# Row maxima at the end of a section: moving a small VectorE step, doubling a temporary and re-timing loads in a fused attention and Fourier kernel

## The chip, the cores and the metric

The kernel runs on one core of a Trainium2 chip. The core has five engines, each with its own in-order instruction stream: TensorE (PE in the profile, with its weight loads as PEld), VectorE (DVE), ScalarE (ACT), GpSimd (POOL) and SyncE (SP, which here only issues DMA transfers). They meet through semaphores. The metric is device time in microseconds (us), the median of several runs.

## The reference

Two branches read the same `x` of 2048 x 512, and a gate mixes them row by row.

```python
g = sigmoid((x * gate_w).sum(-1))
a = dft_seq_re @ (x @ dft_hid_re.T) - dft_seq_im @ (x @ dft_hid_im.T)   # Fourier branch
q, k, v = split(x @ wqkv)                     # 32 heads of 16
b = softmax(q @ k.T / 4) @ v @ wo             # attention branch
out = g * a + (1 - g) * b
```

All of it is fp32. The inputs `wqkv` and `wo` are scaled up by 64, so that scores are large and softmax needs the true maximum of each row.

## The kernel before, in words

**Precision.** Products that need fp32 accuracy are made of three fp32r products: each operand is split into a high part (a cast to fp32r) and a low part (the value minus the high part).

**Attention.** Heads go in 16 pairs `p`; the queries of a pair go in two halves `hf` of 1024. A pair's `q` and `k` lie as two stacks of 64 rows in SBUF (`qs`, `ks`, two buffers each, used by even and odd pairs), loaded from DRAM by `load_stacks(p)`: for each of the two heads one transfer of zeros (more for the first pairs) and six transfers of 16 rows. Rows 48 and 49 of a stack hold the high and low part of the negated row maximum, which thus enters the score through the product itself. So every score tile is made twice. First `a_tile` (L290, L292) makes a tile of 128 queries x 512 keys, and VectorE reduces it to a maximum per query. When all 64 tiles of a pair's half are done, two functions go into the list `deferred`: `m_parts` (L301, L304, L305) reduces the four maxima per query to one (`nm`) and splits it into high and low (`nhl`: a cast, then a subtraction); `m_rows` (L309, L315) transposes them and sends them with eight small DMAs to rows 48 and 49 of the stack, four on the SP queue and, in most halves, four on the POOL queue. Later `scores` (L786, L787) makes the tile the other way round, keys x queries, with the maximum in it, and ScalarE takes the exponential into `pt`. `pv` (L828) multiplies with the values into the bank `acc`; where a section ends, `evacuate` copies `acc` (ScalarE) to the tile `few` and adds it on POOL into `total` (L807, L808).

**Fourier.** The second DFT (`dft`, L461) runs 3072 half-height products whose matrices come in chunks `craw` (L435), split by POOL into `ch` and `cl` (L445, L446). Chunk loads, splits, and the `y`, `yr` transfers of finished tiles are issued from `dft_next`, behind the product after which they become possible.

**Order.** The order on each engine is written by hand. A `segment` (called section in the text) walks through a pattern of slots. In the main stage, here called the full stage, the pattern is `FULL`: sixteen slots, each with a half-height DFT product beside a half-height score product of the other half of the array, eight of them `a` and eight `s`, with bank numbers, and then two steps of `pv`.

```python
FULL = "a5 s4 a2 s0 a3 s6 a5 s4 s1 s0 s2 a6 a3 a4 s5 a1 | |"
```

Bank 6 is the bank of `acc`: the `a6` of slot 11, the fifth maximum tile of the section, is reduced before the section's value products may write there. Before the full stage the sections follow `START` and `THIN`, after it `NINE`. `deferred` is emptied one function at a time: in a FULL section at slot 8 (the condition `n == 8`) and at the section's end; in other sections at the end, and in `NINE` also at the first `|`.

Side work hangs on a plan: `at(u, f)` runs `f` when `u` units (a unit is one key tile of a pair's half, two per section) of values are done. It holds `load_stacks(p)` at 32 (p - 1), and `block`, which fetches four finished pairs of a half and their reciprocal sums (`no`, L596, L598), multiplies them (L610, POOL), splits the product (L614, L615, POOL) and stores it (`oh`, L616), all in three steps at 16, 20 and 22 units after the last pair, and the same 8 units later for the second part. At the end `load_w15` fetches some rows of `wo`.

Of the kernel before, what the change touches and what calls it, by code (L numbers as in the profile page):

```python
# [9 lines left out]
F32 = mybir.dt.float32  # L10
F32R = mybir.dt.float32r
AF = mybir.ActivationFunctionType
ALU = mybir.AluOpType
AX = mybir.AxisListType

P = 128
S = 2048
D = 512
# [13 lines left out]
def mix_kernel(ctx: ExitStack, tc: tile.TileContext, xa_t, xa, wqkv, w_hid, w_seq, wo, gate_w, out):  # L32
# [5 lines left out]
    nc = tc.nc  # L38
# [55 lines left out]
    nm = [const.tile([P, 16], F32, name=f"nm{i}") for i in range(2)]  # L94
# [4 lines left out]
    acc = psO.tile([P, 512], F32, "acc")  # L99
# [161 lines left out]
    qs = [main.tile([P, S], F32R, name=f"qs{i}", tag=f"qs{i}") for i in range(2)]  # L261
    ks = [main.tile([P, S], F32R, name=f"ks{i}", tag=f"ks{i}") for i in range(2)]

    def load_stacks(p):
        q_t, k_t = qs[p % 2], ks[p % 2]
        for h in range(2):
            rows = slice((2 * p + h) * DH, (2 * p + h + 1) * DH)
            o = 64 * h
            if p:
                n = 64 if p < 3 else 50  # L270
                nc.sync.dma_start(q_t[o + 48:o + n].bitcast(F32), z_d[:n - 48])
                if p < 3:
                    nc.sync.dma_start(k_t[o + 50:o + 64].bitcast(F32), z_d[:14])

            for i, (qv, kv) in enumerate(((0, 0), (0, 1), (1, 0))):
                part = slice(o + 16 * i, o + 16 * i + 16)
                nc.sync.dma_start(q_t[part].bitcast(F32), qk_d[0][qv, rows])
                nc.sync.dma_start(k_t[part].bitcast(F32), qk_d[1][kv, rows])


    deferred = []
    a_left = {}

    def a_tile(i, h, ps=None, bank=None):
        p, j = divmod(i, 64)
        qt, kb = divmod(j, 4)
        if ps is None:
            ps = psA.tile([P, 512], F32, "a", bank)
        r = slice(64 * h, 64 * h + (64 if p else 48))
        nc.tensor.matmul(ps, qs[p % 2][r, qt * P:(qt + 1) * P], ks[p % 2][r, kb * 512:(kb + 1) * 512],  # L290
                         start=True, stop=True)
        user = nc.vector.tensor_reduce(mx[p % 2][:, h, qt, kb:kb + 1], ps, AX.X, ALU.max)  # L292
        hf = j // 32
        a_left[p, hf] = a_left.get((p, hf), 64) - 1
        if not a_left[p, hf]:
            deferred.extend((partial(m_parts, p, hf), partial(m_rows, p, hf)))
        return user

    def m_parts(p, hf):

        nc.vector.tensor_reduce(nm[hf].rearrange("p (q h) -> p h q", h=2), mx[p % 2][:, :, 8 * hf:8 * hf + 8, :],  # L301
                                AX.X, ALU.max, negate=True)
        t = nhl[hf]
        nc.vector.tensor_copy(t[:, 0], nm[hf])  # L304
        nc.vector.tensor_tensor(t[:, 1], nm[hf], t[:, 0].bitcast(F32), ALU.subtract)  # L305

    def m_rows(p, hf):

# [17 lines left out]
    nc.gpsimd.memset(zeros, 0.0)  # L326
    nc.gpsimd.memset(vt[:, :, :, 16:17], 1.0)
    load_stacks(0)
    wos = [staged(wo[:, kt]) for kt in range(KT)]
    for i in range(2):  # L330
# [93 lines left out]
    work = ctx.enter_context(tc.tile_pool(name="work", bufs=1, side="right", reuse_waits="tile"))  # L424
# [223 lines left out]
    few = work.tile([P, D], F32, name="few")  # L648
# [43 lines left out]
    w15 = []  # L692

    def load_w15():
        w = work.tile([P, 2, D], F32R, name="w15")
        for i in range(8):
            nc.sync.dma_start(w[16 * i:16 * i + 16].bitcast(F32), wo_d[3][64 * (i % 2) + 3:64 * (i % 2) + 64:4])
        w15.append(w)
# [72 lines left out]
    total = None  # L771
# [17 lines left out]
    def pv_last(u):  # L789
# [6 lines left out]
        if blk == 0 and k2 == 7:  # L796
            last_pairs.append(LastPair(0, [(psS, "s"), (psA, "a")]))
            last_pairs[0].copy(1)

    def evacuate(p, hf, done):  # L800

        nonlocal total
        if total is None:
            total = work.tile([P, 512], F32, name="oe", bufs=2)
            nc.scalar.copy(total, acc)
        else:
            nc.scalar.copy(few, acc)  # L807
            nc.gpsimd.tensor_tensor(total, total, few, ALU.add)  # L808
        if done:
            for qb in range(2):  # L810
                nc.sync.dma_start(o_d[hf][p, :, qb * 512:(qb + 1) * 512], total[64 * qb:64 * qb + 64])
            total = None
# [36 lines left out]
    def issue(x, half, stop=True):  # L849
        chain, st, mv, after, last = x  # L850
        i = chain.mm(st, mv, half, last and stop)
        if stop and after:
            after()
        return i
# [12 lines left out]
    def at(u, f, *args):  # L867
        plan.setdefault(u, []).append(partial(f, *args))

    for hf in range(2):  # L870
        for ct in range(4):
            n = 3 if hf and ct == 3 else 4
            last = 32 * (4 * ct + n - 1) + 16 * (hf + 1)
            at(last + (4 if ct < 3 else 2), sums, hf, ct, n)
            at(last + (12 if ct < 3 else 4), inverse, hf, ct, n)
            if ct < 3:
                for half in range(2):
                    for step, du in enumerate((16, 20, 22)):
                        at(last + du + 8 * half, block, step, hf, ct, half)

    for p in range(1, NP):
        at(32 * (p - 1), load_stacks, p)
    one, two, three = [(psD, "d")], [(psS, "s"), (psD, "d")], [(psS, "s"), (psA, "a"), (psD, "d")]
    at(456, load_yg, 0, range(3))
    at(481, load_yg, 0, range(3, 8))
# [2 lines left out]
    for step, u in ((0, 498), ("sums", 500), (1, 504), (2, 506)):  # L888
        at(u, last_block, step, 0, 4, nc.gpsimd)
    at(498, load_w15)  # L890
    lead = a_next

# [11 lines left out]
    FULL = "a5 s4 a2 s0 a3 s6 a5 s4 s1 s0 s2 a6 a3 a4 s5 a1 | |"  # L904
# [14 lines left out]
    users, valued, exponentials = [], 0, []  # L919

    def score(kind, h, number=None):
        x = next(streams[h][kind == "a"], None)
        if x:
            users.append((kind, a_tile(*x, bank=number) if kind == "a" else scores(*x, number=number)))
            if kind == "s":
                exponentials.append(users[-1][1])

    def values(close=False):
        nonlocal valued
        i = pv(valued, close)  # L930
        valued += 1
        return i

    def segment(pattern, half, ds, stop):


        nonlocal users
        before, users = users, []
        ds, turned = iter(ds), False
        for n, slot in enumerate(pattern.split()):  # L940
            number = None
            if n == 8 and pattern == FULL and deferred:
                deferred.pop(0)()
            if slot[1:].isdigit():
                slot, number = slot[0], int(slot[1])
            if slot == "|":
                end = n == len(pattern.split()) - 1
                i = values(end and (pattern == FULL or valued == thin))
                if end and pattern == FULL:

                    tc.add_manual_dep(i.ins, exponentials[-2].ins.name,
                                      mybir.DependencyInfo(mybir.DependencyClass.Sync, mybir.DependencyReason.DATA))
                while between:
                    between.pop(0)()
                if deferred and pattern in NINE and not turned and "|" in pattern.split()[n + 1:]:
                    deferred.pop(0)()
                    turned = True
                continue
            if not n and number is not None:

                score(slot, 1 - half, number)
            if len(slot) == 1:
                x = next(ds, None)
                if x:

                    before = before if x[0].begun else None
                    i = issue(x, half, stop)
                    users = []
                    if before:
                        tc.add_manual_dep(  # L970
                            i.ins, dict(before).get("s", before[0][1]).ins.name,
                            mybir.DependencyInfo(mybir.DependencyClass.Sync, mybir.DependencyReason.DATA))
                        before = None
            if slot != "-" and (n or number is None):
                score(slot[-1] if slot[0] == "+" else slot[0], 1 - half, number)
            if len(slot) == 2 and slot[0] != "+":
                score(slot[1].lower(), half)

        if deferred and not (pattern in NINE and (turned or len(deferred) == 1)):
            deferred.pop(0)()  # L980

# [16 lines left out]
    pump(hid, 12)  # L998
    ds = take(hid, 12)
    segment(START[0], 0, ds, False)  # L1000
    pump(hid, 12)
    segment(START[1], 1, ds, True)
    values()
    values()
    for patterns, ds in pairs():
        for half in range(2):
            run_plan(valued)
            pattern = FULL if patterns is FULL else patterns[half]
# [69 lines left out]
```

## Time and profile before

| | |
|---|---|
| Median of 3 runs | 1703.19 us (1702.84 to 1703.92) |
| Profiled execution | 1702.28 us, its span 1700.5 us |
| TensorE busy | 1666.7 us, 98% |
| VectorE busy | 1397.7 us, 82% |
| ScalarE busy | 1242.7 us, 73% |
| POOL busy | 656.9 us, 39% |
| Row-maximum tile reductions (L292) | 2026 from `a` banks, mean 683 ns, and 22 from `acc` |
| Row-maximum steps (L301, L304, L305) | 32, of these 24 in the full stage |

Times in the timeline are microseconds from the span's start. A row of the timeline is: start, length, engine, line, operation, output and inputs, shapes, and the number of merged instructions; in square brackets stands how long the engine was idle before it, and who ended that. In the chain of work that ended last a row is start, length, and what ran. In the waits, a row gives total, number of times, longest. Busy times of TensorE are modelled from starts, since its products are pipelined, so its 98% doesn't mean that it runs at its peak.

### The profile page before, as it was taken

What the parts mean: (1) busy time and instruction counts of PE and PEld (TensorE: products, weight loads), DVE (VectorE), ACT (ScalarE), POOL (GpSimd) and SP (SyncE); (2) the same over time, 40 slices, a digit from 0 to 9 for tenths busy, and PEclk for the clock granted to TensorE, in tenths of its full rate; (3) what the DMA queues carried; (4) which work ended last, traced back from release to release, by engine and by line L of the source; (5) the groups of instructions that cost most, each with busy time, mean ns of one, the idle gap of its engine ahead of it and who ended that gap; (6) DMA issues with size and microseconds to landing.
All of it is one profiled execution on the core that took longest, in us unless ns stands there. A gap on an engine that the chain in (4) does not pass through costs nothing.

```text
span 1700.5 us, 34533 instructions
## 1 busy us (share of the span) xinstructions
PE 1666.7 (98%) x13040; PEld 1014.8 (60%) x13040; DVE 1397.7 (82%) x2353; ACT 1242.7 (73%) x2423; POOL 656.9 (39%) x672
## 2 busy tenths in 40 slices
PE   9999999999999999999999999999999999999998
PEld 7888855555565556555556555665555555655444
DVE  5439888888888888888888888888888888889854
ACT  5212377777788778777788777877778787788786
POOL 0201112334444456444444465544445465421110
PEclk9999999999999999999999999999999999999999
DMA  9963600414141433314156434314141535452014
GB/s 289 345 150 131 169 11 2 68 33 83 56 77 46 78 109 90 77 43 83 39 95 243 96 101 108 75 54 86 51 83 62 104 101 114 137 182 44 22 44 138
DMA packets 82688, 166.69 MB, mean 98 GB/s; under 512 B 19664, under 2 KB 20158, under 8 KB 78510
## 3 DMA queue, kind: packets, MB, share of 16 engines
q1 hardware_dynamic: 78282, 163.53, 37.7%
q8 instruction: 103, 1.69, 0.4%
q0 software_dynamic: 3808, 0.30, 0.2%
q14 instruction: 63, 0.52, 0.1%
q10 hardware_dynamic: 432, 0.66, 0.1%
HBM read 109.14 MB, written 54.65 MB: 96 GB/s over the span
## 4 chain that ended last, share of the span: by engine, by line
PE 90%; DVE 7%; DMA 2%; issue 0%; POOL 0%; SPq 0%; ACT 0%; DVEq 0%; POOLq 0%
PE acc L828 27%; PE d L461 21%; PE a L290 16%; PE s L786 14%; DVE mx L292 5%; PE s L375 3%; PE s L407 1%; DVE nhl L304 1%; PE acc L794 1%; PE d L375 1%; DMA ks<-qk 1%; DMA craw<-w_seq 1%; PE s L108 1%; PE a L108 1%; PE a L107 1%; PE s L107 1%
## 5 line engine op out<-in xcount | busy, mean ns | idle before, releaser
L292 DVE TENSOR_REDUCE mx<-a 128x1 f32<-128x512 f32 x2026 | 1258.2, 683 | 193.5 <-PE a L290 166.9
L787 ACT ACTIVATE pt<-s 128x512 f32<-128x512 f32 x2006 | 1023.1, 623 | 70.7 <-PE s L786 57.9
L290 PE MATMUL a<-ks,qs 64*128 64x512 f32 (+1 forms) x2026 | 726.3, 404 | 1.1 <-DVE mx L292 1.1
L786 PE MATMUL s<-qs,ks 64*128 64x512 f32 (+1 forms) x2006 | 690.8, 401 | 3.1 <-ACT few L807 3.1
L461 PE MATMUL d<-xab,ch 64*128 64x512 f32 x2016 | 645.7, 395 | 0.0
L828 PE MATMUL acc<-pt,vt 128*17 128x512 f32 (+1 forms) x3968 | 486.6, 598 | 21.7 <-DVE mx L292 21.7
L290 PEld LDWEIGHTS a<-ks,qs 64*128 64x128 f32 (+1 forms) x2026 | 366.4, 184 | 221.3 <-issue 139.8
L808 POOL TENSOR_TENSOR oe<-oe,few 128x512 f32<-128x512 f32 x169 | 218.3, 1292 | 491.3 <-ACT few L807 483.0
L786 PEld LDWEIGHTS s<-qs,ks 64*128 64x128 f32 (+1 forms) x2006 | 365.1, 185 | 65.2 <-issue 16.8
L461 PE MATMUL d<-xab,cl 64*128 64x512 f32 x1008 | 398.3, 395 | 0.0
L461 PEld LDWEIGHTS d<-xab,ch 64*128 64x128 f32 x2016 | 366.8, 184 | 26.5
L807 ACT COPY few<-acc 128x512 f32<-128x512 f32 x169 | 99.1, 587 | 209.5 <-PE acc L828 200.7
L828 PEld LDWEIGHTS acc<-pt,vt 128*17 128x17 f32 (+1 forms) x3968 | 91.6, 101 | 236.7 <-issue 151.6
L461 PEld LDWEIGHTS d<-xab,cl 64*128 64x128 f32 x1008 | 185.8, 184 | 13.2
L446 POOL TENSOR_TENSOR cl<-craw,ch 128x512 fp32r<-128x512 f32 x126 | 162.3, 1288 | 10.1
L445 POOL CAST ch<-craw 128x512 fp32r<-128x512 f32 x126 | 76.9, 611 | 55.9 <-PE s L786 20.3
L461 PE MATMUL d<-wre,xab 64*128 64x512 f32 x336 | 91.4, 404 | 0.0
L461 PEld LDWEIGHTS d<-wre,xab 64*128 64x128 f32 x336 | 58.7, 185 | 38.3 <-issue 23.3
L315 POOL DMA_DIRECT2D qs<-mt x119 | 67.0, 568 | 33.4 <-PE a L290 12.1
L461 PE MATMUL d<-wo_hl,o_hl 64*128 64x512 f32 (+1 forms) x246 | 69.0, 410 | 0.0
L479 POOL CAST xab<-y 128x512 fp32r<-128x512 f32 x16 | 9.8, 611 | 138.9 <-ACT y L477 95.4
L461 PEld LDWEIGHTS d<-wo_hl,o_hl 64*128 64x128 f32 (+1 forms) x246 | 42.1, 185 | 29.8 <-issue 12.2
(170 smaller groups left out, 1055.3 us busy)
## 6 DMA issues: line engine op xcount, KB each, us to landing
craw<-w_seq SPq DMA_DIRECT2D x128, 256.0 KB
qk<-hl SPq DMA_DIRECT2D x32, 512.0 KB
qs<-qk SPq DMA_DIRECT2D x96, 128.0 KB
ks<-qk SPq DMA_DIRECT2D x96, 128.0 KB
b<-hl SPq DMA_DIRECT2D x16, 512.0 KB
xab<-b SPq DMA_DIRECT2D x16, 512.0 KB
o<-oe SPq DMA_DIRECT2D x62, 128.0 KB
oh<-nh SPq DMA_DIRECT2D x12, 512.0 KB
```

What stands on the lines that cost most here:

```text
L290: nc.tensor.matmul(ps, qs[p % 2][r, qt * P:(qt + 1) * P], ks[p % 2][r, kb * 512:(kb + 1) * 512], start=True, stop=True)
L292: user = nc.vector.tensor_reduce(mx[p % 2][:, h, qt, kb:kb + 1], ps, AX.X, ALU.max)
L315: (nc.gpsimd if own else nc.sync).dma_start(rows.rearrange("v (q b c) -> v b q c", q=8, b=4)[:, b], mt[hf][32 * b + h:32 * b + 32:2])
L375: i = nc.tensor.matmul(ps, st[r], mv[r], start=not half and not j, stop=half == 1 and j == 11)
L445: nc.gpsimd.tensor_copy(h1, raw)
L446: nc.gpsimd.tensor_tensor(l1, raw, h1.bitcast(F32), ALU.subtract)
L461: i = nc.tensor.matmul(self.ps, st[r], mv[r], start=not self.begun, stop=stop)
L786: nc.tensor.matmul(ps, ks[p % 2][rr, kt * P:(kt + 1) * P], qs[p % 2][rr, q0:q0 + 512], start=True, stop=True)
L787: return nc.scalar.activation(pts[u][:, 2 * qb + h], ps, AF.Exp, bias=0.0, scale=DH ** -0.5)
L807: nc.scalar.copy(few, acc)
L808: nc.gpsimd.tensor_tensor(total, total, few, ALU.add)
L828: i = nc.tensor.matmul(acc[32 * j:32 * j + width], v[:, 16 * h:16 * h + width], pt[:, j], start=begin, stop=done or close)
```

## The change

Four edits are made together.

1. In FULL sections both deferred functions, `m_parts` and `m_rows`, are run at the section's end; the place at slot 8 is gone. In these sections the high part is made on VectorE by a `tensor_tensor` that takes the maximum of `nm` with itself, in place of a cast. In all other sections the cast and the subtraction are issued on POOL.
2. `evacuate` copies `acc` into two temporaries in turn, `part[0]` and `part[1]`, in place of the one tile `few`. They lie in the buffer that `w15` takes at the end.
3. `load_stacks` is called for one head at a time; the second head of a pair is fetched 2 units after the first (not for the first call, `p` = 1).
4. The three steps of `block` are planned 4 units later: 20, 24 and 26.

```diff
-    def load_stacks(p):
+    def load_stacks(p, heads=range(2)):
         q_t, k_t = qs[p % 2], ks[p % 2]
-        for h in range(2):
+        for h in heads:
...
         t = nhl[hf]
-        nc.vector.tensor_copy(t[:, 0], nm[hf])
-        nc.vector.tensor_tensor(t[:, 1], nm[hf], t[:, 0].bitcast(F32), ALU.subtract)
+        if full_now:
+            nc.vector.tensor_tensor(t[:, 0], nm[hf], nm[hf], ALU.max)
+        else:
+            nc.gpsimd.tensor_copy(t[:, 0], nm[hf])
+        (nc.vector if full_now else nc.gpsimd).tensor_tensor(t[:, 1], nm[hf], t[:, 0].bitcast(F32), ALU.subtract)
...
     def load_w15():
-        w = work.tile([P, 2, D], F32R, name="w15")
+        part.clear()
+        w = work.tile([P, 2, D], F32R, name="w15", tag="w15")
...
         else:
-            nc.scalar.copy(few, acc)
-            nc.gpsimd.tensor_tensor(total, total, few, ALU.add)
+            if not part:
+                two = work.tile([P, 2, 512], F32, name="part", tag="w15")
+                part.extend(two[:, i] for i in range(2))
+            part.reverse()
+            nc.scalar.copy(part[0], acc)
+            nc.gpsimd.tensor_tensor(total, total, part[0], ALU.add)
...
-                    for step, du in enumerate((16, 20, 22)):
+                    for step, du in enumerate((20, 24, 26)):
                         at(last + du + 8 * half, block, step, hf, ct, half)
 
     for p in range(1, NP):
-        at(32 * (p - 1), load_stacks, p)
+        for h in range(2):
+            at(32 * (p - 1) + 2 * h * (p > 1), load_stacks, p, [h])
...
     def segment(pattern, half, ds, stop):
-        nonlocal users
+        nonlocal users, full_now
+        full_now = pattern == FULL
...
-            if n == 8 and pattern == FULL and deferred:
-                deferred.pop(0)()
...
+        while full_now and deferred:
+            deferred.pop(0)()
         if deferred and not (pattern in NINE and (turned or len(deferred) == 1)):
             deferred.pop(0)()
```

More of the change, by code (lines that the diff above doesn't have):

```diff
@@ L281, in mix_kernel @@
     deferred = []
+    full_now = False
     a_left = {}
@@ L798, in pv_last @@
             last_pairs[0].copy(1)
+    part = []
     def evacuate(p, hf, done):
```

## The prediction

> **What bounds the kernel now.** I read the page first, for the engines' shares and the chain that ended last; then the timeline of VectorE and of TensorE, section by section; then the row-maximum tiles, POOL and the chain in order of time.
>
> ```profile
> span 1700.5 us, 34533 instructions
> PE 1666.7 (98%) x13040; PEld 1014.8 (60%) x13040; DVE 1397.7 (82%) x2353; ACT 1242.7 (73%) x2423; POOL 656.9 (39%) x672
> ...
> PE 90%; DVE 7%; DMA 2%; issue 0%; POOL 0%; SPq 0%; ACT 0%; DVEq 0%; POOLq 0%
> ```
>
> TensorE is the bound, with VectorE in the chain for 7%. Where VectorE enters shows in its timeline; each full section is one row of eight reductions (L292, one per score tile).
>
> ```profile
> 601.30 2.48 DVE L292 TENSOR_REDUCE mx<-a 128x1 f32<-128x512 f32 x4 [0.68 <-PE a L290]
> 603.82 0.22 DVE L301 TENSOR_REDUCE nm<-mx 128x16 f32<-128x64 f32 x1
> 604.07 0.82 DVE L304 CAST nhl<-nm 128x16 fp32r<-128x16 f32 x1
> ...
> 605.37 2.47 DVE L292 TENSOR_REDUCE mx<-a 128x1 f32<-128x512 f32 x4
> ...
> 608.49 5.04 DVE L292 TENSOR_REDUCE mx<-a 128x1 f32<-128x512 f32 x8 [0.53 <-PE a L290]
> ...
> 648.77 2.48 DVE L292 TENSOR_REDUCE mx<-a 128x1 f32<-128x512 f32 x4 [0.71 <-PE a L290]
> ...
> 655.00 5.04 DVE L292 TENSOR_REDUCE mx<-a 128x1 f32<-128x512 f32 x8 [0.53 <-PE a L290]
> 660.76 5.04 DVE L292 TENSOR_REDUCE mx<-a 128x1 f32<-128x512 f32 x8 [0.72 <-PE a L290]
> ...
> 695.37 2.48 DVE L292 TENSOR_REDUCE mx<-a 128x1 f32<-128x512 f32 x4 [0.72 <-PE a L290]
> ...
> 702.23 5.04 DVE L292 TENSOR_REDUCE mx<-a 128x1 f32<-128x512 f32 x8 [0.53 <-PE a L290]
> ```
>
> An ordinary section lasts 5.76 us (655.00 to 660.76) and leaves VectorE 0.72 us idle at its end. One section in eight also carries the row-maximum step (L301, L304, L305) between its fourth and fifth reduction, and lasts 7.19 us (601.30 to 608.49), 6.23 (648.77 to 655.00) or 6.86 (695.37 to 702.23). The step delays the fifth reduction, whose bank the value products (L828) accumulate into next, so TensorE waits. The three lengths come from the cast:
>
> ```profile
> L304 DVE CAST nhl<-nm x32: 174/784/836, 172.4 to 1636.9; 128x16 fp32r<-128x16 f32 x32
> L305 DVE TENSOR_TENSOR nhl<-nm,nhl x32: 174/176/518, 172.6 to 1637.5; 128x16 fp32r<-128x16 f32 x32
> ```
>
> ```profile
> 603.57 1.29 POOL L446 TENSOR_TENSOR cl<-craw,ch 128x512 fp32r<-128x512 f32 x1
> ```
>
> A cast of 16 columns takes 174 ns at best and 784 in the median. The one at 604.07 ended at 604.89, 0.03 after POOL's subtraction (604.86): it waited for POOL.
>
> Two of these sections are longer still:
>
> ```profile
> 975.14 1.92 PE L828 MATMUL acc<-pt,vt 128*32 128x512 f32 x16
> 983.91 1.93 PE L828 MATMUL acc<-pt,vt 128*32 128x512 f32 x16 [0.78 <-DVE mx L292]
> ```
>
> ```profile
> 363.64 1.85 PE acc L828 x16
> ...
> 962.70 6.68 DMA ks<-qk
> 969.46 6.72 DMA craw<-w_seq
> ...
> 1490.56 1.85 PE acc L828 x16
> ```
>
> ```profile
> 976.30 0.61 POOL L445 CAST ch<-craw 128x512 fp32r<-128x512 f32 x1 [7.37 <-DMA craw<-w_seq]
> ```
>
> ```profile
> 979.54 0.58 ACT L807 COPY few<-acc 128x512 f32<-128x512 f32 x1 [3.49 <-POOL oe L808]
> ```
>
> 8.77 us from products to products. The DFT chunk `craw` was issued behind fourteen stack loads and landed late, POOL stood 7.37 us, its addition that frees `few` came late, and ScalarE stood 3.49 us. The second, four head pairs later, looks the same.
>
> Summed over the full stage: 24 sections with the step, twelve near 1.10 above 5.75, four near 1.44, six near 0.49, two near 3.05: 13.2 + 5.8 + 2.9 + 6.1 = 28.0 us. Check: from 363.64 to 1490.56 are 191 sections, 1126.92 us, against 191 x 5.75 = 1098.3 (28.7 over; 26.8 with 5.76). So nothing but these 24 sections is over.
>
> **The change, part by part.** The sum is made against the profiled execution, 1702.28 us (its span of 1700.5 and 1.8 around it), 0.9 below the median of 1703.19.
>
> *Step at the section's end, max in place of the cast (24 sections).* Removed from mid-section: everything that makes the 28.0. Added behind the eighth reduction: L301 (0.22), the max, the subtraction, then the transposition that stands there already and takes 0.19 of the idle time (0.72 against 0.53). No max of 16 columns is in the trace; its nearest row is L305, the same form and size: 0.17, or 0.52 where POOL holds it up. I take 0.17. With three gaps of 0.03 that is 0.19 + 0.22 + 0.17 + 0.17 + 0.09 = 0.84 against 0.72: the next section's first reduction starts 0.12 late. Does that reach TensorE?
>
> ```profile
> 803.77 1.44 DVE L292 TENSOR_REDUCE mx<-a 128x1 f32<-128x512 f32 x2
> ```
>
> ```profile
> 805.31 0.64 PE L828 MATMUL acc<-pt,vt 128*32 128x512 f32 x4
> ```
>
> These are the fourth and fifth reductions of an ordinary section. Back to back they run 0.60 apart (2.48 for four of 0.68), so the fifth could end at 803.77 + 0.60 + 0.68 = 805.05; it ended at 805.21, having waited for its matmul, and the products followed 0.10 later, where a delayed fifth is followed in 0.05. About 0.2 us in hand covers 0.12. Without the cover each section costs 0.12, 3 us in all.
>
> The row transfers (L315; eight issues a step, four on POOL behind its addition) leave the 0.7 us later that the transposition comes; the maxima are gathered several sections before they are read.
>
> *What POOL still does to the step.* Where the DFT's second half ends a chain, POOL works at the section's end:
>
> ```profile
> 1031.02 1.92 PE acc L828 x16
> ```
>
> ```profile
> 1032.70 0.61 POOL L445 CAST ch<-craw 128x512 fp32r<-128x512 f32 x1
> ```
>
> Counted from the start of a section's products, the eighth reduction ends at 1.70 (805.21 + 3 x 0.60 = 807.01, against 805.31), so the max is due at 1.96; this cast runs from 1.68 to 2.29, and a max that waits for it ends at 2.32, not 2.13. That is 0.19 late on top of the 0.12, of which the 0.2 in hand leaves about 0.1. By the instruction order of the changed kernel four or five of the 24 are like this, and in one a delayed block product pushes POOL's work back, so that the max and the subtraction both wait: 1.3 late, 1.1 after the cover. Residue: 1.1 + 5 x 0.1, and some rounding: 2.0. Full stage: 28.0 - 2.0 = 26.0 gained.
>
> *Two temporaries, halved stacks, later blocks.* The 2 x 2.0 us of the long sections beyond 1.1 are in that 28.0. In the new order `craw` stands behind seven stack loads, not fourteen and four block loads: about 5 us earlier, and a late addition finds a second buffer. All other full sections are level, so these edits gain nothing there. Their cost: the second half's seven issues move one section behind the first's (5.75 later, in place of seven issues of about 0.5, so some 2.3 us), past `craw`, `yr` and sometimes an `oh` store on SP.
>
> ```profile
> 968.60 0.30 SPq L278 DMA_DIRECT2D ks<-qk  x1
> ```
>
> ```profile
> 985.77 0.50 PE L290 MATMUL a<-ks,qs 64*128 64x512 f32 x1
> ```
>
> The last stack load of pair 9 was issued at 968.60, lands in about 6.7, and its first user runs at 985.77: 10.5 in hand, 8 after the change. Zero. Blocks move by two sections on queues with room; they are read hundreds of us later. Zero.
>
> *Step outside the full stage (8 of 32): cast and subtraction on POOL.*
>
> ```profile
> 230.28 1.05 PE L828 MATMUL acc<-pt,vt 128*17 128x512 f32 x8
> 234.76 1.05 PE L828 MATMUL acc<-pt,vt 128*17 128x512 f32 x8
> 236.88 1.05 PE L828 MATMUL acc<-pt,vt 128*17 128x512 f32 x8
> 240.48 1.05 PE L828 MATMUL acc<-pt,vt 128*17 128x512 f32 x8
> ...
> 1502.28 1.05 PE L828 MATMUL acc<-pt,vt 128*17 128x512 f32 x8
> 1506.19 1.05 PE L828 MATMUL acc<-pt,vt 128*17 128x512 f32 x8
> ...
> 1513.79 1.05 PE L828 MATMUL acc<-pt,vt 128*17 128x512 f32 x8
> 1517.11 1.05 PE L828 MATMUL acc<-pt,vt 128*17 128x512 f32 x8
> ```
>
> ```profile
> 238.34 0.20 DVE L309 STREAM_TRANSPOSE mt<-nhl 128x32 f32<-128x32 f32 x1
> ```
>
> Before the full stage three steps cost 4.48 - 3.60 = 0.88 each, where they put 1.1 on VectorE; only L301 with its gap (0.25) remains, about what is absorbed today. Gain 3 x 0.85 = 2.6 (bounds 0 and 2.6). After it, three cost 3.91 - 3.32 = 0.59 for 0.6 on VectorE; 0.25 remains: gain 3 x 0.3 = 0.9 (0 to 1.8). The two others, at 172 and 1637: 0.2 and 0. POOL's price for 16 columns is not in the trace; it lies between nothing and the 512-column rows, 0.61 + 1.29 = 1.9, and the transposition that waits for it comes 3.6 us after the products of its section began (238.34 against 234.76). Only at 1637 does it follow at once: 0 to 1.9, and what it feeds is read some steps later. I take 0.
>
> Sum: 26.0 + 2.6 + 0.9 + 0.2 = 29.7 us. 1702.3 - 29.7 = 1672.6; on the median's level 1673.5. Forecast: **1673 us**.
>
> **The rivals.**
> *The wait moves along with the step.* The max reads SBUF twice and, like L305 at its 518 ns, can be held up by a POOL instruction. A full wait of 1.29 per section, less 0.1 still in hand, gives 1.2; in all 24 sections that is 29 and the time about 1702, in half 14 and 1687. For it: the row above. Against: in most of these sections POOL's row ends before the step would begin. Chance 0.09.
> The Trainium skill (SBUF — State Buffer, the section "SBUF: two separate sides") says that a VectorE instruction with two SBUF inputs takes the port pair shared with GpSimd against a GpSimd instruction that reads SBUF, as a two-port copy does. By that rule swapping the cast for a max avoids nothing, and only the place can help; the 518 ns agree.
>
> *The two long sections stay*, because another load takes the place of the stacks ahead of `craw` (the blocks now follow them): 2 x 2.0 back, 1677. Chance 0.11.
>
> *POOL is slow with the small operations* outside the full stage and gives those 3.7 back: 1676 to 1677. Chance 0.05.
>
> *Slower: the second half stack comes too late.* It now stands on SP behind `craw`, whose issue waits for POOL.
>
> ```profile
> SPq L435 <- POOL cl L446: 431.6, 98, 11.1
> ```
>
> These waits run up to 11.1 us. Past the 8 in hand, each microsecond stops TensorE once for each of 14 pairs: at 10.1 late the 29.7 are used up, at 11.1 the time is 1673 + 14 x 3.1 = 1716. Against: most such waits end before the second half is due at all. Chance 0.04.
>
> **How the numbers follow.** Forecast 0.71, rivals 0.09, 0.11, 0.05, 0.04. A measurement of this kernel can tell about 0.2%, 3.4 us, from no change; only the last rival and the far end of the first are not faster: faster 0.94, same 0.02, slower 0.04. Range: below, all excess gone (28.0 + 2.6 + 1.8 + 0.4 = 32.8): 1670, a little less for scatter, 1668. Above: the long sections stay and half a dozen steps wait: 1673 + 4 + 6 x 1.2 = 1684.
>
> **What would show it.** Right: sections with the step at 5.75 to 5.9, the new max near 0.17, no row of L828 that waits over 0.5 for VectorE, no 8.8 us section, ScalarE never waiting for POOL's addition. Wrong: a max of 0.5 or more in many sections; TensorE or VectorE waiting for `ks` or `qs` loads; new sections of 7 us or more where blocks meet `craw`.

## The result and the profile after

The changed kernel takes 1674.97 us (median of 4 runs, 1674.52 to 1675.48) against 1703.28 us for the kernel before on the same chip (1702.84 to 1703.92): a ratio of 0.9834, with a 95% interval of 0.9817 to 0.9851. The forecast was 1673, its range 1668 to 1684. The profiled execution took 1675.2 us, its span 1673.4, which is 27.1 less than before.

Lines have moved by the edits: what was L290, L292, L301, L304, L305, L309, L828 is now L291, L293, L302, L306, L309, L313, L839. Of the page of the changed kernel, the span, the engines' shares and the chain by engine:

```profile
span 1673.4 us, 34595 instructions
PE 1663.6 (99%) x13040; PEld 1023.8 (61%) x13040; DVE 1383.1 (83%) x2337; ACT 1242.9 (74%) x2423; POOL 660.1 (39%) x688
...
PE 98%; DVE 1%; DMA 0%; ACT 0%; issue 0%; DVEq 0%
```

VectorE's busy time fell by only 14.6 us (1397.7 to 1383.1), but its share of the chain that ended last fell from 7% to 1%. TensorE is now 98% of that chain. The full stage lost 22.2 us, counted from its first full value products to its last:

```profile
359.92 1.92 PE L839 MATMUL acc<-pt,vt 128*32 128x512 f32 x16
...
1464.67 1.92 PE L839 MATMUL acc<-pt,vt 128*32 128x512 f32 x15
```

These are TensorE's timeline rows that answer to the chain rows at 363.64 and 1490.56 before: 1104.75 us against 1126.92. The first of them also comes 3.7 us earlier, which is the gain ahead of the full stage, and the rest, 27.1 - 22.2 - 3.7 = 1.2, lies behind it.

The step at its new place, in VectorE's timeline of the changed kernel:

```profile
597.93 0.21 DVE L302 TENSOR_REDUCE nm<-mx 128x16 f32<-128x64 f32 x1
598.17 0.26 DVE L306 TENSOR_TENSOR nhl<-nm 128x16 fp32r<-128x16 f32 x1
598.47 0.18 DVE L309 TENSOR_TENSOR nhl<-nm,nhl 128x16 fp32r<-128x16 f32 x1
598.77 0.21 DVE L313 STREAM_TRANSPOSE mt<-nhl 128x32 f32<-128x32 f32 x1
598.91 4.87 DVE L293 TENSOR_REDUCE mx<-a 128x1 f32<-128x512 f32 x8
...
604.50 5.05 DVE L293 TENSOR_REDUCE mx<-a 128x1 f32<-128x512 f32 x8 [0.26 <-PE a L291]
```

The step now stands between two rows of eight reductions, in the time that was idle. The section's own row of eight is whole again (4.87 us, without an idle gap in it), and the products that follow this step came 5.77 us after those before it, against 7.19 for the corresponding section before.

The row-maximum operations, by tile (duration in ns: least, median, most):

```profile
L306 DVE TENSOR_TENSOR nhl<-nm x24: 174/175/1041, 367.6 to 1431.0; 128x16 fp32r<-128x16 f32 x24
L309 DVE TENSOR_TENSOR nhl<-nm,nhl x24: 174/175/519, 367.8 to 1432.1; 128x16 fp32r<-128x16 f32 x24
L308 POOL CAST nhl<-nm x8: 190/196/209, 171.9 to 1610.3; 128x16 fp32r<-128x16 f32 x8
L309 POOL TENSOR_TENSOR nhl<-nm,nhl x8: 220/222/223, 172.2 to 1610.6; 128x16 fp32r<-128x16 f32 x8
```

The median of the first is 175 ns where the cast had 784. But the longest max took 1041 ns, more than any cast before. And POOL's small operations cost 0.20 and 0.22 us, together about a fifth of the 1.9 us that the prediction had to set as their bound.

In the waits of the changed kernel (total, times, longest), the weight loads of the value products still wait for VectorE in every section, but by 0.4 at most, and ScalarE's copy waits for the products, by 1.3 at most:

```profile
ACT part L818 <- PE acc L839: 181.1, 166, 1.3
PEld acc L839 <- DVE mx L293: 62.5, 192, 0.4
PE a L291 <- DVE mx L293: 2.2, 4, 0.6
```

Before, the second of these waits was 84.8 us with 1.8 at most, and the value products on TensorE itself waited another 21.7 us for VectorE. The third row is the larger one now (1.1 us before); the next paragraph shows where its four waits come from. No section near 8.8 us is left.

**Where 6.0 us stayed.** The 24 sections with a step exceed 5.75 us by 6.0 in sum, where 28.0 were and 2.0 were expected. Sixteen are over by 0.01 to 0.08 (0.7 in sum), three by 0.22 to 0.26 (their max takes 0.37 to 0.38, until POOL's subtraction L450 ends), one by 0.41, and four by 1.02 to 1.07 (4.2 in sum). One of the four, in the timeline of the changed kernel:

```profile
1011.40 1.93 PE L839 MATMUL acc<-pt,vt 128*32 128x512 f32 x16
1012.96 1.28 POOL L524 TENSOR_TENSOR y<-y,yr 128x512 f32<-128x512 f32 x1
1013.24 1.04 DVE L306 TENSOR_TENSOR nhl<-nm 128x16 fp32r<-128x16 f32 x1
1014.19 0.61 POOL L449 CAST ch<-craw 128x512 fp32r<-128x512 f32 x1
1014.31 0.52 DVE L309 TENSOR_TENSOR nhl<-nm,nhl 128x16 fp32r<-128x16 f32 x1
1014.86 0.21 DVE L313 STREAM_TRANSPOSE mt<-nhl 128x32 f32<-128x32 f32 x1
...
1018.22 1.92 PE L839 MATMUL acc<-pt,vt 128*32 128x512 f32 x16
```

POOL adds a finished Fourier tile (L524, 1012.96 to 1014.24). The max is due at 1013.24 and ends at 1014.28, 0.04 after it. Then POOL's next cast begins at 1014.19, and the subtraction takes 0.52 in place of 0.17. Max and subtraction both wait, 0.87 + 0.35 = 1.22 late, so the reductions behind them are late too, a product of a later maximum tile waits for the bank that they empty (one of the four waits above), and the section lasts 6.82 us.

Sixteen sections are not quite at 5.75 either. Two rows of the same view show why:

```profile
552.30 0.17 DVE L309 TENSOR_TENSOR nhl<-nm,nhl 128x16 fp32r<-128x16 f32 x1
552.71 0.21 DVE L313 STREAM_TRANSPOSE mt<-nhl 128x32 f32<-128x32 f32 x1 [0.23 <-DVE nhl L309]
```

The transposition starts 0.23 us after the subtraction ends, where the prediction reckoned 0.03. Between the two, the trace has four separate wait instructions of VectorE for the transposition's output buffer, which the last row transfers must have left; they are not counted as busy:

```
EVENT_SEMAPHORE L313   552.317
EVENT_SEMAPHORE L313   552.415
EVENT_SEMAPHORE L313   552.513
EVENT_SEMAPHORE L313   552.611
STREAM_TRANSPOSE L313  552.707
```

One takes about 0.1 us, though nothing was left to wait for: the semaphores that these four read had last changed 20 us before or earlier. Before, the same waits stood at 652.26 to 652.55, early in a section and 1.7 us ahead of their transposition (654.28), with reductions in between, so they cost nothing that showed.

### The profile page after: what moved, and what is told of

Same layout as the page of the kernel before. It is cut to its first block, busy times and chain, and to the rows that moved or that the text cites. A ratio compares the mean times of both kernels' runs of the same rounds, so it can differ in the third digit from the quotient of the medians.

```text
span 1673.4 us, 34595 instructions
## 1 busy us (share of the span) xinstructions
PE 1663.6 (99%) x13040; PEld 1023.8 (61%) x13040; DVE 1383.1 (83%) x2337; ACT 1242.9 (74%) x2423; POOL 660.1 (39%) x688
## 4 chain that ended last, share of the span: by engine, by line
PE 98%; DVE 1%; DMA 0%; ACT 0%; issue 0%; DVEq 0%
PE acc L839 27%; PE d L465 27%; PE a L291 17%; PE s L791 14%; PE s L379 3%; PE s L411 1%; PE acc L799 1%; PE d L379 1%; PE s L106 1%; PE a L106 1%; PE a L108 1%; PE s L108 1%; PE s L107 1%; PE a L107 1%; DVE mx L293 1%; PE s L465 1%
## 5 line engine op out<-in xcount | busy, mean ns | idle before, releaser
L293 DVE TENSOR_REDUCE mx<-a 128x1 f32<-128x512 f32 x2026 | 1256.5, 683 | 177.3 <-PE a L291 151.8
L291 PE MATMUL a<-ks,qs 64*128 64x512 f32 (+1 forms) x2026 | 726.7, 405 | 2.2 <-DVE mx L293 2.2
L291 PEld LDWEIGHTS a<-ks,qs 64*128 64x128 f32 (+1 forms) x2026 | 366.3, 184 | 217.2 <-issue 128.7
L839 PE MATMUL acc<-pt,vt 128*17 128x512 f32 (+1 forms) x3968 | 486.7, 598 | 0.0
L819 POOL TENSOR_TENSOR oe<-oe,part 128x512 f32<-128x512 f32 x169 | 218.3, 1292 | 507.7 <-ACT part L818 502.6
L818 ACT COPY part<-acc 128x512 f32<-128x512 f32 x169 | 99.2, 587 | 183.0 <-PE acc L839 181.1
L839 PEld LDWEIGHTS acc<-pt,vt 128*17 128x17 f32 (+1 forms) x3968 | 91.6, 101 | 214.3 <-issue 151.5
L450 POOL TENSOR_TENSOR cl<-craw,ch 128x512 fp32r<-128x512 f32 x126 | 162.1, 1286 | 10.1
L465 PEld LDWEIGHTS d<-wo_hl,o_hl 64*128 64x128 f32 (+1 forms) x246 | 42.3, 185 | 29.7 <-issue 12.1
```

The lines of the kernel that those rows point to most:

```text
L450: nc.gpsimd.tensor_tensor(l1, raw, h1.bitcast(F32), ALU.subtract)
L465: i = nc.tensor.matmul(self.ps, st[r], mv[r], start=not self.begun, stop=stop)
L818: nc.scalar.copy(part[0], acc)
L819: nc.gpsimd.tensor_tensor(total, total, part[0], ALU.add)
L839: i = nc.tensor.matmul(acc[32 * j:32 * j + width], v[:, 16 * h:16 * h + width], pt[:, j], start=begin, stop=done or close)
```

## Experiments

"Over" below is by how much the sections of the full stage exceed 5.75 us in one profiled execution, summed over those with a step and those clearly longer than 5.75: 28.0 before, 6.0 after the change. Each ratio is to the kernel before on the same chip, with its 95% interval.

### The place or the operation

Two kernels split the first edit. One keeps the max and puts the step back into the middle of the section; the other keeps the place and goes back to the cast.

```diff
+            if n == 8 and pattern == FULL and deferred:
+                deferred.pop(0)()
...
-        while full_now and deferred:
-            deferred.pop(0)()
```

> The whole change, but in full sections the step is back at slot 8, with the max in place of the cast. Theory (the place is what counts, and the max waits for POOL like the cast): 14 sections at 1.1, 4 at 1.44 and 6 at 0.5 over the ordinary one, 24 us, against 6.0 in the changed kernel: about 1693 us. Rival (the operation is what counts): the max runs in 0.17 everywhere, each section is over by 0.5 as those with a short cast were, 12 us: about 1681 us.

```diff
-            nc.vector.tensor_tensor(t[:, 0], nm[hf], nm[hf], ALU.max)
+            nc.vector.tensor_copy(t[:, 0], nm[hf])
```

> The whole change, but the high part is made by the cast, as before, at the section's end. Theory (place): as the changed kernel, 1675 us, within 1. Rival (operation): the cast waits at the section's end too and in more sections than the max, 0.5 to 1.2 us in a third of them or more: 1679 to 1690 us.

Max in the middle: 1692.13 us, 0.9940 (0.9924 to 0.9957), 23.5 over. Cast at the end: 1674.91 us, 0.9840 (0.9825 to 0.9855), 6.1 over. The tile's rows, first of the max in the middle, then of the cast at the end:

```profile
L306 DVE TENSOR_TENSOR nhl<-nm x24: 191/824/897, 366.0 to 1446.6; 128x16 fp32r<-128x16 f32 x24
```

```profile
L306 DVE CAST nhl<-nm x24: 174/175/1042, 367.6 to 1431.0; 128x16 fp32r<-128x16 f32 x24
```

In the middle, the max waits as the cast did in the kernel before (824 ns in the median against 784). At the end the cast is as quick as the max, and waits in the same sections. In the middle the max gains nothing either: with the same loads and temporaries, the old cast there leaves 23.5 us over as well (the second run of the next section). So the operation is worth nothing, and the place everything. The Trainium skill (SBUF — State Buffer, the section "SBUF: two separate sides") has it that a VectorE instruction with two SBUF inputs takes the port pair that it shares with GpSimd against a GpSimd instruction that reads SBUF, just as a copy does. These rows agree: 824 ns beside POOL's work, 174 clear of it.

### The step alone, and the other three edits alone

> The moved step alone: row maxima at the section's end with the max, POOL outside the full stage; one temporary, whole stacks, blocks at 16, 20 and 22 as before. Theory: the step is worth all but the two long sections, and these need the other three edits; they come back with about 2 us each, so about 1679 us against 1675 for the whole change. Rival: the long sections were long only because a delayed section met a late addition; without the delay they are ordinary, and the time is 1675.

> The other three edits alone: two temporaries, stacks in halves, blocks 4 units later, with the old step (cast and subtraction on VectorE, at slot 8). Theory: only the two long sections shrink to some 1.1 us of excess, about 1699 us against 1703.3. Rival: the edits move the stall elsewhere or were never the cause, 1703.

The first undoes edits 2, 3 and 4; the second has these and the old step. Step alone: 1682.86 us, 0.9885 (0.9870 to 0.9900), 13.5 over. The others alone: 1696.70 us, 0.9966 (0.9955 to 0.9978), 23.5 over. The first missed by 4 us upwards, the second by 2 downwards. In the kernel with the step alone, the 24 sections with a step are over by 6.0, as in the whole change. The other 7.5 lie in two sections without a step, 3.60 and 3.87 over. The timeline of the kernel with the step alone, at the first of the two:

```profile
960.72 0.61 POOL L449 CAST ch<-craw 128x512 fp32r<-128x512 f32 x1 [7.63 <-DMA craw<-w_seq]
...
963.95 0.58 ACT L814 COPY few<-acc 128x512 f32<-128x512 f32 x1 [3.74 <-POOL oe L815]
...
964.59 0.49 PE L791 MATMUL s<-qs,ks 64*128 64x512 f32 x1 [1.78 <-ACT few L814]
...
968.66 2.20 PE L835 MATMUL acc<-pt,vt 128*32 128x512 f32 x16
```

It is the stall that the prediction found: a late chunk, POOL waiting 7.63, ScalarE 3.74, and then TensorE 1.78 for a score's bank. In the kernel before, the step stood in the same section as this stall and took its delay in the shadow of it, 3.03 and 3.08 over in all. The prediction had split those as 1.1 for the step and 2.0 for the stall. With the step gone the stall shows in full: it was worth 3.6 to 3.9 by itself, and the step there nothing. (POOL's wait is also 0.26 us longer in this run than before, so the two sizes are not quite alike.)

With the other three edits alone, the two long sections fall from 3.03 and 3.08 to 0.84 and 0.83, and that is all but 0.1 of the 4.5 us by which the sum over falls; smaller shifts in the other sections cancel. The full stage of that run also begins 1.2 us earlier than before the change. Of this, 1.05 us is there already where the first row-maximum step begins (171.09 against 172.14 us), before any of the edits acts. In two traces of the changed kernel itself it begins at 171.65 and 171.16 us, and in all 14 traces between 171.1 and 172.6, so most of the 1.2 is scatter of the start.

### Which of the three edits removes that stall

Three kernels have the step's edit and one of the others: the two temporaries, the halved stacks, or the later blocks. Each undoes two of these:

```diff
-            part.reverse()
-            nc.scalar.copy(part[0], acc)
-            nc.gpsimd.tensor_tensor(total, total, part[0], ALU.add)
+            nc.scalar.copy(few, acc)
+            nc.gpsimd.tensor_tensor(total, total, few, ALU.add)
...
-                    for step, du in enumerate((20, 24, 26)):
+                    for step, du in enumerate((16, 20, 22)):
...
-        for h in range(2):
-            at(32 * (p - 1) + 2 * h * (p > 1), load_stacks, p, [h])
+        at(32 * (p - 1), load_stacks, p)
```

> The moved step and the two temporaries, with whole stacks and the blocks as before. Theory: the two long sections are ScalarE's wait for the one temporary; with a second one it is gone, 1675 us, though the chunk still lands late. Rival: POOL is so late that both temporaries are taken, and more than half of the 7.5 us that the two sections cost with the step alone stays: 1679 to 1683.

> The moved step and the stacks in halves, with one temporary and the blocks as before. Theory: the chunk load stands behind seven stack loads less and lands some 3 us earlier, so that about 3 of each section's 3.7 us go: 1676 us. Rival: the four block loads and the first half hold it as long: 1680 or more.

> The moved step and the later blocks, with one temporary and whole stacks. Theory: the chunk load still stands behind fourteen stack loads; only the four block loads ahead of them (2.6 us of issues) and a block product on POOL are out of the way: about 2 of each section's 3.7 us go, 1679 us. Rival: the blocks' work on POOL was the cause: 1675.

With the temporaries 1676.26 us, 0.9843 (0.9828 to 0.9857), 7.6 over; with the stacks 1675.30, 0.9836 (0.9821 to 0.9851), 5.9 over; with the blocks 1675.27, 0.9836 (0.9822 to 0.9851), 6.0 over. Any one of the three does the whole work of the three, within about 1 us. For the first two that is near what was expected. For the later blocks 1679 was expected, and the number of its rival came out. How they do it differs, as POOL's wait for the chunk shows (total, times, longest): first with the temporaries, then with the stacks, then with the blocks.

```profile
POOL ch L449 <- DMA craw<-w_seq: 19.8, 3, 7.3
```

```profile
POOL ch L449 <- DMA craw<-w_seq: 0.8, 1, 0.8
```

```profile
POOL ch L449 <- DMA craw<-w_seq: 5.9, 1, 5.9
ACT few L814 <- POOL oe L815: 4.1, 3, 1.5
```

The halved stacks remove the wait. With the later blocks the 5.9 is a wait elsewhere, at 1236 us, which the kernel with the step alone has too (5.91) and which costs nothing. At the first of the two places POOL now stands 5.95 in place of 7.63, and the trace puts that down to TensorE and no longer to the chunk:

```profile
957.57 0.61 POOL L449 CAST ch<-craw 128x512 fp32r<-128x512 f32 x1 [5.95 <-PE s L791]
```

This split begins some 3 us sooner than with the step alone (960.72), and ScalarE waits for the products alone. At the second place ScalarE waits 1.53 for POOL's addition, and the section is 0.2 over. The rival, that the blocks' work on POOL was the cause, doesn't fit the rows of the step alone, though its number came out: ScalarE's wait of 3.74 ended at 963.95 with the addition, while the block's cast on POOL started at 963.86, behind that addition. The temporaries leave the wait as it is (7.3) and take ScalarE out of it; POOL's backlog then meets two steps (0.28 and 1.12 over, where the changed kernel has 0.01 and 0.02), which is where the extra 1.4 us is.

### POOL for the steps outside the full stage

```diff
-            nc.gpsimd.tensor_copy(t[:, 0], nm[hf])
-        (nc.vector if full_now else nc.gpsimd).tensor_tensor(
+            nc.vector.tensor_copy(t[:, 0], nm[hf])
+        nc.vector.tensor_tensor(
```

> The whole change, but outside the full stage the cast and the subtraction stay on VectorE. Theory: the three steps before the full stage lose their 0.9 us again, the three after it 0.4, the first one 0.4 at most: 3.9 to 4.3 us, 1679 us. Rival: these steps were hidden and the gain there came from elsewhere: 1675.

1679.61 us, 0.9861 (0.9845 to 0.9878): as expected. Timeline rows of the value products around the second such step, of the changed kernel, and then of this one:

```profile
229.39 1.05 PE L839 MATMUL acc<-pt,vt 128*17 128x512 f32 x8
232.94 1.05 PE L839 MATMUL acc<-pt,vt 128*17 128x512 f32 x8
```

```profile
229.39 1.05 PE L839 MATMUL acc<-pt,vt 128*17 128x512 f32 x8
233.86 1.05 PE L839 MATMUL acc<-pt,vt 128*17 128x512 f32 x8
```

3.55 us with the cast and the subtraction on POOL, 4.47 with them on VectorE, at the same place. With POOL the step costs nothing there (the section at 240.79, without a step, takes 3.55 too), although the first reduction of the step is still on VectorE.

### Waiting past POOL's addition

The four sections at 1.05 should go if the step waited for the end of the next section, where POOL has other work.

```diff
+        due = len(deferred)
...
-        while full_now and deferred:
+        for _ in range(due if full_now else 0):
             deferred.pop(0)()
-        if deferred and not (pattern in NINE and (turned or len(deferred) == 1)):
+        if not full_now and deferred and not (pattern in NINE and (turned or len(deferred) == 1)):
```

> The whole change, but in full sections the step waits for the end of the section after the one that ends the maxima: the other half of the pair of sections, in which no DFT chunk is split and no y tile is added. Theory (the 6.0 us that are left in the full stage are POOL instructions that hold up the max and the subtraction): the four sections at 1.05, the one at 0.41 and the three at 0.24 become like the others, 0.05 to 0.1; the row transfers leave 5.75 us later, which the 8 us between their landing and the first score that reads them cover: 1670 us. Rival: the rest is the longer tail of VectorE itself or the later transfers stop TensorE: 1675 or more.

1674.93 us, 0.9833 (0.9816 to 0.9849): no better than the change, a miss of 5 us. The long waits for POOL did go (the max takes 360 ns at most, the subtraction 177), but two others came. In the timeline of this kernel, VectorE at one of seven steps that are over by 0.37 to 0.47, and TensorE in a section that is over by 1.44:

```profile
558.89 0.21 DVE L313 STREAM_TRANSPOSE mt<-nhl 128x32 f32<-128x32 f32 x1 [0.23 <-DVE nhl L309]
559.03 0.52 DVE L582 RECIPROCAL rc<-rc 128x64 f32<-128x64 f32 x1
559.47 3.07 DVE L293 TENSOR_REDUCE mx<-a 128x1 f32<-128x512 f32 x5
...
891.17 0.47 PE L791 MATMUL s<-qs,ks 64*128 64x512 f32 x1 [0.99 <-DMA qs<-mt]
```

The reciprocal of the sums is planned for just that section's end, and it makes the step half a microsecond longer, in six of the seven; the seventh has a gap of 0.58 us ahead of its transposition instead. And one score comes to wait for the rows of maxima, which the later step sends later.

To test the first of these readings, the reciprocal was moved one section on, with the changed kernel run beside it on the same chip:

```diff
-            at(last + (12 if ct < 3 else 4), inverse, hf, ct, n)
+            at(last + (14 if ct < 3 else 4), inverse, hf, ct, n)
```

> The whole change, with two things added: every row-maximum step of a full section waits for the end of the section after the one in which its maxima are complete, and the reciprocal of the sums is planned two units (one section) later, at 14 in place of 12, so that it no longer stands right behind the transposition. With the step waiting alone, eight sections were over by 0.37 to 0.47 with the reciprocal in them, and one by 1.44 where a score waited for a row transfer; the sum over was 5.7 us. Theory (the eight are the reciprocal's): they fall to under 0.1 each, the one of 1.44 stays, the sum over falls to about 2.5 us and the time to 1671.7. Rival (the eight come from the later place of the step itself): they stay, and the time is 1674.9. Second rival: the moved reciprocal now meets something else, a score or another step, and makes new long sections of its own; then the eight are gone, but the sum over stays at 4 us or more.

> The changed kernel as it is, beside the other kernel of this call on the same chip, as the measure for it: 1675.0 by its earlier runs, and 3.3 us slower than the kernel with the step one section later and the reciprocal moved, if that one's theory holds; equal to it within 1 us if the first rival holds.

1672.53 us (1672.31 to 1673.29), 0.9824 (0.9811 to 0.9838), against 1674.50 (1674.29 to 1674.91), 0.9836 (0.9823 to 0.9849) for the changed kernel beside it: 2.0 us faster, where the theory had 3.3. The expectation spoke of eight, by counting one of 0.24 in. The six with a reciprocal fall to below 0.1, so these were the reciprocal's. The one with the gap of 0.58 stays, at 0.44, and so does the one of 0.24. The score's wait stays and is a little longer (1.23, its section 1.70 over). One section with the moved reciprocal is over by 0.36, so the second rival has a small part. 3.8 us remain over.

Last, the step waits only in the second half of the full stage, where the four additions meet it, and the reciprocals move too:

```diff
+        due = len(deferred)
+        late = valued >= thin + 1 + 4 * NT * 3
...
-        while full_now and deferred:
+        for _ in range((due if late else len(deferred)) if full_now else 0):
             deferred.pop(0)()
...
-            at(last + (12 if ct < 3 else 4), inverse, hf, ct, n)
+            at(last + (14 if ct < 3 else 4), inverse, hf, ct, n)
```

> The whole change, and two things more: in the second half of the full stage, from its unit 246 on, the step waits for the end of the next section, as in the earlier run, and the reciprocals of the sums are planned 2 units later, so that they no longer stand behind the step. Theory: the waits for POOL's y additions (four of 1.05, one of 0.41) go, the reciprocals' 0.4 does not come in their place, and the one late transfer of the earlier run (1.4) stood in the first half: 4.3 us less, about 1671 us. Rival: other instructions or transfers meet the step there: 1673 to 1675.

1671.76 us (1671.19 to 1672.15), 0.9814 (0.9800 to 0.9829), 1.9 over: the lowest median of all, near the expected 1671, though its interval overlaps that of the kernel before it. It wasn't run beside the changed kernel; their times don't overlap, while the kernel before agreed within 0.5 us beside each (1703.77 and 1703.28). Its timeline at the step that was shown at 1013.24 above and now comes one section later:

```profile
1019.62 0.36 DVE L306 TENSOR_TENSOR nhl<-nm 128x16 fp32r<-128x16 f32 x1
1020.01 0.17 DVE L309 TENSOR_TENSOR nhl<-nm,nhl 128x16 fp32r<-128x16 f32 x1
1020.38 0.21 DVE L313 STREAM_TRANSPOSE mt<-nhl 128x32 f32<-128x32 f32 x1 [0.20 <-DVE nhl L309]
```

The max and the subtraction that took 1.04 and 0.52 take 0.36 and 0.17 there.

## Why the prediction was right, and where it was off

The forecast of 1673 missed the median of 1674.97 by 2 us, and its reason held: the mid-section step delayed the fifth reduction, and the place at the end took that away. The number came out somewhat better than the full stage did: that gained 3.8 us less than forecast, and 1.2 us more elsewhere made up for part of it, about 0.5 of this probably luck (the scatter of the start, below). By its own terms, from the two profiled executions:

| Term | predicted | measured |
|---|---|---|
| Ahead of the full stage | 2.6 + 0.2 | 3.7 |
| Full stage | 26.0 | 22.2 |
| After it | 0.9 | 1.2 |
| Sum | 29.7 | 27.1 |

*The full stage's 28.0.* The sum was right, and all of it was the 24 sections. Its split was not: the two long sections were not 1.1 for the step and 2.0 for the late chunk, but nearly all the chunk's stall. That changes nothing in the sum, since both went, but it makes the three other edits worth 7.5 us (13.5 - 6.0) beside the new step where 4.0 stood, so that the price of the rival in which those sections stay was too low (1677 where the run without the edits took 1682.9).

*The residue of 2.0 is the term that failed*: 6.0. The step that failed in it is "in one a delayed block product pushes POOL's work back, so that the max and the subtraction both wait", with five others at 0.1. Its price was right (1.1; the rows give 1.02 to 1.07), but it occurs four times, and a block product isn't its cause. What the max meets is POOL's addition of a finished Fourier tile, which starts when ScalarE has handed over the tile `y`. It stands right ahead of the cast at 1032.70 from which the prediction reckoned. Here it is before the change, where the products came at 1031.02, and after it at the second of the four places, where they came at 1150.58 and no block is near:

```profile
1031.48 1.28 POOL L520 TENSOR_TENSOR y<-y,yr 128x512 f32<-128x512 f32 x1 [1.36 <-ACT y L519]
```

```profile
1152.13 1.29 POOL L524 TENSOR_TENSOR y<-y,yr 128x512 f32<-128x512 f32 x1 [1.29 <-ACT y L523]
1152.43 1.02 DVE L306 TENSOR_TENSOR nhl<-nm 128x16 fp32r<-128x16 f32 x1
```

In all four sections the addition began 0.45 to 0.47 us after the products before the change and 1.53 to 1.56 after them now. The prediction placed POOL's work by its distance from the products in the profile before, and there the products themselves were delayed by 1.1 us, by the step that was to be moved. With TensorE on time, the addition lands just where the max now stands. Only the first of the four (1011.40) has a block product on POOL ahead of it, and in the kernel with the moved step and the halved stacks, whose blocks come as before, that product is gone and the same section is 1.08 over all the same. A tile's chain ends every six sections and a step comes every eight, so every third step of the second half of the full stage meets an addition. These four make up 4.2 of the 6.0 us. The milder case was reckoned as a max that waits for POOL's cast, 0.19 late; it is one that waits for POOL's subtraction, 0.20 late (0.37 against 0.17). It occurs three times and leaves 0.24, not 0.1, since the time in hand was used up already (next point). So the rival in which the wait moves along was right in kind, in four sections of 24.

*The step's own 0.84* left out the four wait instructions ahead of the transposition. Its start comes 0.41 after the subtraction's start, where 0.20 was reckoned. That is 0.2 more beside the 0.12, though the next reduction starts a little sooner behind the transposition (0.13 after its start; 552.84 in VectorE's timeline). The "about 0.2 us in hand" covered nearly all of it: 0.01 to 0.08 remain in sixteen sections.

*The max in place of the cast* was taken at 0.17 by the nearest row: 0.175 in the median. That the operation avoids nothing, said in the prediction's sentence on the port, is shown by the two runs that part it from the place.

*POOL's small operations* were taken at zero cost between 0 and 1.9 us. They take 0.20 + 0.22, and the gain is 0.9 in each of three sections ahead of the full stage (0.85 predicted) and 0.4 in each of three after it (0.3). The 0.9 that came on top before the full stage lies ahead of the first of these sections. Half of it is there before the step at 172 us begins (171.65 against 172.14), and two traces of the changed kernel differ by as much at that point (171.65 and 171.16), so this half can't be told from scatter of the start. The other half is gained at that step, where 0.2 was expected.

*The second half stack* was in no danger: no wait of TensorE or of its weight loads for `ks` or `qs` from `qk` is in the waits of the changed kernel. Between the last landing and the first use lie 5.8 to 8.5 us, somewhat less than the 8 that were reckoned from one pair.

*What stays open*: in one section of the changed kernel (products at 1203.74, 0.41 over) 0.45 us pass from the first of the four wait instructions to the second. A single such gap shows in ten of the 14 traces, the 0.58 above among them, not always at the same step. It has one mark in all ten: it follows VectorE's recorded instruction number 1854 or 1214 (counted from 0, five times 128 apart), and 1.1 to 1.4 us later an 8 KB transfer of an instruction queue begins. So it may belong to the loading of VectorE's instructions. But in the kernel with the max in the middle a wait instruction with the number 1854 shows no such gap, and no run tried it.

## What to carry to other kernels

A small operation that slows an engine costs by its place, not by its kind: find the idle time that the in-order engine has in each period, and count everything that the moved step issues, separate wait instructions included, against it. When placing it, work out where the neighbour's work will stand after the stall is gone, not where it stands in the profile before; here POOL's addition kept its place while the products beside it came 1.1 us earlier. Two stalls in one section overlap, so that the price of one is known only with the other taken away, and several cures of one stall don't add up.

## What was not expected of the hardware

- A VectorE max, cast or subtraction of 16 columns takes 0.17 us alone, and up to 1.04 us when it meets a POOL instruction that runs already. In the changed kernel all 12 that were held up end 0.03 to 0.04 us after the POOL instruction. Where POOL's next instruction has begun by then, the next VectorE operation is held up once more (0.52 us against 0.17).
- The reduction to 16 columns just ahead of them (L302), which reads one operand, was never held up: 0.21 to 0.22 us in all 32 places, though in 15 of them a POOL instruction ran all the while.
- POOL's cast and subtraction of 128 x 16 elements take 0.20 and 0.22 us.
- Each separate wait instruction on VectorE takes about 0.1 us although what it waits for is long done. The profile's busy times don't show them; the idle time in front of the transposition does.
